# The first feed-forward product of three tile pairs as seven block products in place of eight

## The chip, the core and the metric

The kernel runs on one core of one Trainium2 chip. The metric is the device time of one execution in microseconds (us). Five engines work side by side, each through a program of its own in fixed order: TensorE (PE; its weight loads are shown as PEld), VectorE (DVE), ScalarE (ACT), GpSimd (POOL) and SyncE (SP, which here issues DMAs). They wait for one another on semaphores. TensorE writes its products to PSUM, eight banks of 128 partitions x 512 float32; the other data lie in SBUF. Lower is better.

## The reference

Attention over normalised queries and keys, a Fourier mixing, a normalisation and a feed-forward layer, for 8 batches of 448 tokens with 12 heads of 64 (768 features, 3072 hidden):

```python
def _attn_ref(q, k, v, tau):
    q_n = q / (np.linalg.norm(q, axis=-1, keepdims=True) + 1e-06)
    k_n = k / (np.linalg.norm(k, axis=-1, keepdims=True) + 1e-06)
    scores = np.matmul(q_n, k_n.transpose(0, 1, 3, 2)) / tau
    ...
    return np.matmul(attn, v).astype(np.float32)

def _moe_ref(x, w_ch1, w_ch2):
    X = np.fft.fft(x, axis=1)
    X = np.fft.fft(X, axis=2)
    mixed = np.real(X).astype(np.float32)
    u = x + mixed
    mu = np.mean(u, axis=-1, keepdims=True)
    var = np.mean((u - mu) ** 2, axis=-1, keepdims=True)
    un = (u - mu) / np.sqrt(var + 1e-06)
    ch = np.maximum(un @ w_ch1, 0.0) @ w_ch2
    return (u + ch).astype(np.float32)
```

The change concerns `un @ w_ch1`, called the first product here; the product with `w_ch2` is the second.

## The kernel before

**Planner.** No instruction is written straight to an engine. Each operation is added to a plan (`Plan.add`, L152) with the engines that may run it, a modelled duration, a priority (a lower number goes first) and the names of the buffers that it reads and writes, from which its dependencies follow. `Plan.schedule` (L196) then puts the operations in order on each engine by list scheduling with these modelled times; `emit` (L366) writes them out with the waits. PSUM is handed out in `Tile`s from two pools: "M", two tiles of one bank, and "G", three tiles of two banks. The table `SHIFT` (L39) adds a correction, found beforehand, to the priority of single operations, so that it shapes the order of the whole program. `fill` puts warm-up matmuls into gaps of TensorE.

**Order of the work.** `build` goes through the batches: Fourier mixing of batch b (`fft`, L1039), then attention of batch b+1 (`attn`, L835), then the feed-forward layer of batch b (`ffn`, L1284). The feed-forward matmuls carry priority 5000 + b and each follows the one before (`self.main`), so they form one chain that fills TensorE wherever attention and mixing leave room. After attention of batch 7 and its mixing only this chain is left.

**Tiles.** The symmetry of the transform leaves three or four tiles of 128 tokens a batch. Odd batches have two pairs, even ones (but batch 0) a pair and a single tile. (b, i) below is the pair of batch b that begins with tile i; the last three pairs are (6,0), (7,0) and (7,2), and between (6,0) and (7,0) comes the single tile of batch 6. The normalised tiles lie transposed in `UNT` (6 blocks of 128 features x 4 slots of 128 tokens), put there by DMA transposes on SP's queue (L1147).

**First product.** `up` (L1179) takes units. For a pair a unit is two hidden blocks of 128, each with 6 matmuls (one for each 128 features) whose moving operand is 256 wide (both tiles), 12 matmuls into one bank; 12 units a pair, 144 matmuls. The relu on the way out of PSUM (L1210, on ACT or DVE) writes the bank to `HQ`, quarters 0 to 3: quarter `h + 2t` is half h of the hidden features of tile t. For a single tile a unit is four hidden blocks of 24 matmuls 128 wide.

**Second product.** It is already done with seven block products in place of eight (Strassen-Winograd): sums of weight blocks in `TX` and in place in `W2b` (`sums`, L1364, made once), sums of quarters of `HQ` on DVE (`comb`, L1316: s1 writes the fifth quarter 4 = 2 + 3, s3 writes 2 = 2 - 0, s2 writes 0 = 4 - 0, s4 writes 1 = 1 - 0, each in three parts k), products m1, m2, m6, m5, m7, m3, m4 of 12 matmuls 384 wide (`prod`, L1218, in three parts c), and `fin` (L1238), which moves partial results to the output staging `OUTB` or adds them there. `store` (L1261) sends `OUTB` out, by SP's queue or by an indirect DMA of POOL (L1278).

**Buffers that the change uses.** `STG` (staged queries and keys), `QH` (the same, normalised), `QT` and `KT` (their transposes), `E` (exponentials) belong to the attention, which has ended for batch 7 when the last pairs are computed.

Of the kernel before, what the change touches and what calls it, by code (L numbers as in the profile page):

```python
# [6 lines left out]

AluOp = mybir.AluOpType
# [7 lines left out]
NJ = DM // 128  # L16
# [23 lines left out]
    "iota": {0: -518.9}, "cst": {0: 1028.3}, "tqd": {1: 36.2}, "vz1": {0: 13.5}, "ldt0": {0: 144.7}, "half": {1: -49}, "ldt": {0: 140.9},  # L40
# [53 lines left out]

LATE = {r"W[12]_\d+": 1.5, "tmd": 2.0, r"sq\d_2": 4.0, r"sq\d_\d": 2.0, r"ktd\d": 3.0, r"qdup\d": 3.0, r"qk\d._[2-7]": 1.5, r"pv\d\d_[2-7]": 2.0, r"pv\d\d_1": 1.0, r"h\d+_[1-7]": 0.3}
PIECE = {r"sc[KQ]\d_0": 0.95, r"scT\d_0": 0.42, r"sc\d_\d": 0.6, r"f[avm]\dp_\d": 0.54, r"t\d\d": 0.94}
PORT = r"eps\d|f[a01]\d_\d|g\d_\d|u\d+_\d|un\d_\d|s\d\d_\d|t\d\d|sc[KQT]\d_\d"  # L100
# [1395 lines left out]
```

## Time and profile before

| | us |
|---|---|
| median of 3 runs | 591.05 (590.52 to 591.43) |
| profiled execution | 588.35 |
| its span, first to last instruction | 586.4 |
| busy: PE, PEld | 566.3, 437.5 |
| busy: DVE, ACT, POOL | 416.9, 353.7, 215.1 |
| granted TensorE clock | 0.999 |

How to read it: a group of instructions is shown with its line in the kernel, engine, operation, output and inputs, shape and count, then busy time and the mean duration of one in ns, then the idle time of the engine before it. Durations of matmuls contain a tail that overlaps the next one, so the pace of a stream is read from the chain of waits, where the pieces don't overlap, and not from a mean duration. A window shows the busy time of each engine between two points of time from the span's start.

### The profile page before, as it was taken

Reading aid. Unit: us, or ns where it says so; the run is one execution under the profiler, and the core shown is the slowest. Engines: PE = TensorE matmul, PEld = TensorE weight load, DVE = VectorE, ACT = ScalarE, POOL = GpSimd, SP = SyncE. Lnnn points to the kernel's source line nnn. Section 1 sums busy time; section 2 is a strip of 40 time slices with the busy share of each in tenths; the row PEclk is TensorE's granted clock in tenths of the full one; section 3 lists DMA queues with packets and bytes.
Section 4 is the critical chain, followed back from the end, with each engine's and each line's share of the span. In section 5 each row is a group of like instructions: output and inputs, shape, how many; then the busy total and the mean of one; then the engine's idle time right before and its main releaser. Section 6 shows DMA issues by size and latency. Waiting matters only on the chain.

```text
span 586.4 us, 14876 instructions
## 1 busy us (share of the span) xinstructions
PE 566.3 (97%) x6070; PEld 437.5 (75%) x6070; DVE 416.9 (71%) x971; ACT 353.7 (60%) x681; POOL 215.1 (37%) x318
## 2 busy tenths in 40 slices
PE   3989999999999999999999999999999999999997
PEld 2668788686686786868778687688868778778684
DVE  8989967997679989795899779857944668112222
ACT  7896986257966795478559766784465334124140
POOL 7734424464373527432352652425210120200302
PEclk9999999999999999999999999999999999999999
DMA  9999999865299659745592599249110011110101
GB/s 220 180 218 167 166 185 117 189 141 107 65 165 113 150 110 148 157 68 123 72 172 49 117 171 100 68 113 167 29 39 31 15 55 33 63 42 1 55 1 55
DMA packets 187637, 62.12 MB, mean 106 GB/s; under 512 B 166704, under 2 KB 185392, under 8 KB 187568
## 3 DMA queue, kind: packets, MB, share of 16 engines
q1 hardware_dynamic: 129648, 38.35, 34.1%
q0 software_dynamic: 57920, 22.81, 31.6%
q8 instruction: 48, 0.79, 0.6%
q14 instruction: 21, 0.17, 0.1%
HBM read 51.90 MB, written 11.01 MB: 107 GB/s over the span
## 4 chain that ended last, share of the span: by engine, by line
PE 83%; DVE 9%; DMA 3%; issue 2%; ACT 1%; POOL 1%; SPq 0%; POOLq 0%; DVEq 0%; ACTq 0%
PE PS L1194 35%; PE PS L1225 31%; PE PS L935 5%; PE PS L898 5%; PE PS L1060 2%; PE PS L929 2%; PE PS L1022 2%; DVE U L1088 1%; DMA TX<-in_q_dram 1%; DMA QT<-QH 1%; PE PS L910 1%; DVE QH L717 1%; DVE HQ L1319 1%; ACT E L876 1%; PE PS L911 1%
## 5 line engine op out<-in xcount | busy, mean ns | idle before, releaser
L1194 PE MATMUL PS<-UNT,W1b 128*128 128x256 bf16 (+1 forms) x2304 | 234.2, 259 | 0.4 <-DMA UNT<-F 0.3
L1194 PEld LDWEIGHTS PS<-UNT,W1b 128*128 128x128 bf16 x2304 | 198.8, 98 | 23.0 <-issue 2.6
L876 ACT ACTIVATE E<-PS 128x900 bf16<-128x900 f32 (+1 forms) x192 | 148.0, 827 | 28.0 <-PE PS L898 25.4
L1210 ACT ACTIVATE HQ<-PS 128x512 bf16<-128x512 f32 x129 | 77.0, 597 | 97.8 <-PE PS L1194 96.9
L1225 PE MATMUL PS<-W2b,HQ 128*128 128x384 bf16 x768 | 133.9, 326 | 0.0
L824 POOL TENSOR_TENSOR QH<-STG,SM 128x256 bf16<-128x256 f32 x126 | 84.0, 694 | 97.8 <-DVE SM L633 72.4
L1225 PEld LDWEIGHTS PS<-W2b,HQ 128*128 128x128 bf16 x768 | 73.5, 98 | 46.4 <-issue 2.2
L1319 DVE TENSOR_TENSOR HQ<-HQ 128x512 bf16<-128x512 bf16 x141 | 62.4, 465 | 48.2 <-ACT HQ L1210 44.9
L1249 POOL TENSOR_TENSOR OUTB<-OUTB,U 128x192 f32<-128x192 f32 x66 | 39.8, 624 | 139.5 <-ACT OUTB L1244 138.7
L1225 PE MATMUL PS<-TX,HQ 128*128 128x384 bf16 x396 | 70.9, 326 | 0.2 <-DVE OUTB L1256 0.2
L1225 PEld LDWEIGHTS PS<-TX,HQ 128*128 128x128 bf16 x396 | 37.8, 98 | 24.2 <-issue 0.7
L817 DVE TENSOR_REDUCE SM<-QH 128x6 f32<-128x384 f32 x84 | 44.8, 541 | 10.1 <-ACT QH L815 9.5
L815 ACT ACTIVATE QH<-STG 128x384 f32<-128x384 f32 x84 | 42.5, 519 | 14.6 <-DVE SM L817 9.9
L935 PE MATMUL PS<-VB,E 128*128 128x65 bf16 x1152 | 50.8, 193 | 0.0
L935 PEld LDWEIGHTS PS<-VB,E 128*128 128x128 bf16 x1152 | 47.5, 97 | 1.0
L1278 POOL DMA_INDIRECT out_dram<-OUTB,IDX x20 | 20.6, 1031 | 64.7 <-issue 33.1
L929 PE MATMUL PS<-VZ,E 128*128 128x130 bf16 x192 | 41.6, 219 | 0.3 <-ACT E L876 0.3
L1088 DVE TENSOR_TENSOR U<-ACG,X 128x384 bf16<-128x384 f32 (+3 forms) x70 | 39.6, 590 | 2.2 <-POOL OUTB L1249 1.4
L898 PE MATMUL PS<-QT,KT 64*128 64x225 bf16 x576 | 40.0, 261 | 1.2 <-ACT E L876 0.7
L1256 DVE TENSOR_TENSOR OUTB<-PS,OUTB 128x384 f32<-128x384 f32 x33 | 18.2, 551 | 30.4 <-PE PS L1225 27.0
L1210 DVE TENSOR_SCALAR HQ<-PS 128x512 bf16<-128x512 f32 x33 | 22.7, 687 | 17.9 <-PE PS L1194 17.9
L898 PEld LDWEIGHTS PS<-QT,KT 64*128 64x128 bf16 x576 | 22.7, 94 | 15.8 <-issue 5.4
(134 smaller groups left out, 623.1 us busy)
## 6 DMA issues: line engine op xcount, KB each, us to landing
STG<-in_k_dram SPq DMA_DIRECT2D x18, 384.0 KB, 4.5
STG<-in_q_dram SPq DMA_DIRECT2D x18, 384.0 KB, 3.9
VB<-in_v_dram POOLq DMA_DIRECT2D x24, 192.0 KB, 7.4
W1b<-in_moe_w_ch_dram POOLq DMA_DIRECT2D x12, 384.0 KB, 7.5
W2b<-in_moe_w_ch_dram POOLq DMA_DIRECT2D x12, 384.0 KB, 6.7
out_dram<-OUTB SPq DMA_DIRECT2D x7, 384.0 KB, 2.6
TX<-in_k_dram SPq DMA_DIRECT2D x2, 576.0 KB, 5.5
TX<-in_q_dram SPq DMA_DIRECT2D x2, 576.0 KB, 7.1
```

Of the source, the lines that this page charges most:

```text
L815: P.add("act", lambda a, sq=sq, src=buf[:, w * x:w * x + w]: a.activation(sq, src, ACTF.Square), t_act(w) + 0.034, pr, f"sq{i}_{b}", reads ...
L817: P.add("dve", lambda v, o=SS[:, i, H // ns * x:H // ns * (x + 1)], sq=sq: v.tensor_reduce(o, sq.rearrange("p (h d) -> p h d", d=DH), AX.X ...
L824: r = v.tensor_tensor(v3(qh)[:, h:h + 4], v3(buf)[:, h:h + 4], RN[:, i, h:h + 4].unsqueeze(2).to_broadcast((128, 4, DH)), AluOp.mult)
L876: return a.activation(o, self.PS[:, bk:bk + nc_, 0:SQ2], ACTF.Exp, scale=1.0 / self.tau)
L898: i = pe.matmul(self.PS[:, bk + h, c0:c0 + NK], self.KT[r, jj, kt * 128:(kt + 1) * 128], self.QT[r, jj, cols], start=True, stop=True)
L929: r = pe.matmul(o, st(6), self.VZ[:, j, :], start=not split, stop=(split and i == 0), skip_group_check=True)
L935: r = pe.matmul(o[:, 65 * h:65 * h + 65], st(2 * kt + h), self.VB[:, kt, 2 * j + h, :], start=(split and i == h == kt == 0), stop=((not sp ...
L1088: return v.tensor_tensor(U[o0:o0 + n, ut, cs].rearrange("p (i e) -> p i e", e=2), src, X[i0:i0 + n, x, cs].rearrange("p (i e) -> p i e", e ...
L1194: r = pe.matmul(self.PS[:, bk, x * n:(x + 1) * n], self.W1b[:, j, ft * 128:(ft + 1) * 128], self.UNT[:, j, cs], start=(j == 0), stop=(j == ...
L1210: return e.activation(o, i, ACTF.Relu) if e is self.nc.scalar else e.tensor_relu(o, i)
L1225: r = pe.matmul(self.PS[:, bk, 0:n], lhs(f), rhs(f), start=(start and f == 0), stop=(stop and f == NF // 2 - 1), skip_group_check=True)
L1319: P.add("dve", lambda v: v.tensor_tensor(cs(o), cs(a), cs(bq), op), 0.335, -0.5, f"{nm}{k}_{b}", reads=rd, writes=hr(o)(k))
```

## The change

In the pairs named in `ROUNDS` the first product is also done with seven block products. The blocks are: activations A[t][k], tile t and half k of the 768 features (3 blocks of 128); weights W[k][h], h half of the hidden features. A round r takes hidden blocks 4r to 4r+3 of each half (the work of four units). Pair (6,0) does rounds 0 and 1 so, and its last four units as before; (7,0) and (7,2) do all three rounds.

- `wsums(r)`: three sums of weight blocks, V0 to V2, of 128 x 1536 in buffers of the attention (round 0 in `STG`, 1 in `QH`, 2 in `KT` and `E[1]`), and a fourth in place in `W1b`. Four DVE operations a round, twelve in all.
- `mixed`: four sums of activation blocks, S0 to S3, in the fifth quarter of `HQ`; then the rounds, interleaved by a written sequence. Each product is 12 matmuls 128 wide. In a round the first bank of a G tile gets a1, then a6, a7 and a4 on top, the second a5 and a3, an M tile a2. Between them the bank is copied out (`copy`, float32, on ACT or DVE) and combined (`add`, a custom DVE operation: sum, clipped at 0) into `HQ`.
- `spare`: the buffers of these copies: `OUTB` in three parts, in batch 7 first three parts of `QT`.
- `ffn`: with three rounds the last two products of the third go behind the first and the third part of m1 (`hook`), and s1, s3 are added there.
- `up`: for the single tile of batch 6 the sum A0 + A1 replaces the second half of the activations where the weight was changed in place; the count of matmuls stays.
- `SHIFT` is replaced as a whole, `PORT` (operations that the planner takes to share a port with POOL) has the new names.

```diff
+ROUNDS = {(6, 0): (0, 1), (7, 0): (0, 1, 2), (7, 2): (0, 1, 2)}
+TPRIO = {0: 610, 1: 611, 2: 620}
...
+        if not pair and self.T3:
+            A = self.UNT[:, 0:3, cs], self.UNT[:, 3:6, cs]
+            self.sa(b, 0, lambda v: v.tensor_tensor(self.SA[:, 0], A[0], A[1], AluOp.add), un, True)
...
+    def sa(self, b, x, fn, rd, first=False):
+
+        self.P.add(("dve", "pool"), fn, (0.267, 0.62), -0.5, f"z{x}0_{b}", reads=rd + ([] if first else self.san),
+                   writes=[f"SA{x}"] + (self.san if first else []))
+
+    def mixed(self, b, idx, rounds):
...
+        self.sa(b, 0, tt(SA[:, 0], A[1][0], A[1][1], AluOp.add), un[1], True)
+        self.sa(b, 1, tt(SA[:, 1], SA[:, 0], A[0][0], AluOp.subtract), ["SA0"] + un[0])
+        self.sa(b, 2, tt(SA[:, 2], A[1][0], A[0][0], AluOp.subtract), un[0] + un[1])
+        self.sa(b, 3, tt(SA[:, 3], A[0][1], SA[:, 1], AluOp.subtract), ["SA1"] + un[0])
...
+            def prod(nm, tl, w, a, start, stop, read=None, acq=None):
+                for f in range(0, 4, 2):
+                    def fn(pe, f=f):
+                        for y in (f, f + 1):
+                            for j in range(3):
+                                i = pe.matmul(ps(tl)[:, 128 * y:128 * y + 128], w[0](y, j), a[0](j), start=(start and y == j == 0),
+                                              stop=(stop and y == 3 and j == 2), skip_group_check=True)
+                        return i
+                    self.main = P.add("pe", fn, 6 * t_mm(128), 5000 + b, f"{nm}{r}_{b}", reads=w[1] + a[1], tiles=(tl[0],),
+                                      acquire=acq if f == 0 else None, after=[self.main] + ([read] if read else []))
+                return self.main
+
+            def copy(nm, tl, op):
+                k = free.pop(0)
+                buf, bn = bufs[k]
+                first = bn[0] not in used
+                used.add(bn[0])
+
+                def ev(e):
+                    return e.activation(buf, ps(tl), ACTF.Copy) if e is self.nc.scalar else e.tensor_copy(buf, ps(tl))
+                c = P.add(("act", "dve"), ev, (t_act(512), t_dve(512)), -1, f"{nm}{r}_{b}", reads=[] if first else bn,
+                          writes=[f"CP{k}"] + (bn if first else []), after=(op,), tiles=(tl[0],))
+                return k, c
+
+            def add(nm, q, tl, k, op):
+                free.append(k)
+                return P.add("dve", lambda v: v._custom_dve(TENSOR_ADD_SAT, out=hq(q), in0=ps(tl), in1=bufs[k][0], s0=3.4028235e38, s1=0.0),
+                             t_dve(512), -1, f"{nm}{r}_{b}", reads=bufs[k][1] + [f"CP{k}"], writes=hn(q), after=(op,), tiles=(tl[0],))
+            op = prod("a1", b1, W(0, 0), U_(0, 0), True, False, acq=g)
+            ka, rd = copy("ca", b1, op)
+            yield
+            op = prod("a2", ta, W(1, 0), U_(0, 1), True, True, acq=ta[0])
+            add("ra", 0, ta, ka, op)
+            yield
+            op = prod("a5", tb, V(0), S(0), True, False)
+            kc, rd2 = copy("cc", tb, op)
+            yield
+            op = prod("a6", b1, V(1), S(1), False, False, rd)
+            kb, rd = copy("cb", b1, op)
+            yield
+            op = prod("a3", tb, W(1, 1), S(3), False, True, rd2)
+            add("rb", 1, tb, kb, op)
+            yield
+            op = prod("a7", b1, W(0, 1), S(2), False, False, rd)
+            rd = add("rc", 3, b1, kc, op)
+            yield
+            op = prod("a4", b1, V(2), U_(1, 1), False, True, rd)
...
+        seq = {1: "u u a a a u a a u a u a u u u", 2: "u a a a b b a a b u a b b a u b u b",
+               3: "a a a b b a a b b a b c a c c b c c b"}[len(rounds)].split()
...
+    def spare(self, b):
...
+        bufs = [(o[:, 512 * x:512 * x + 512], ["OUT0", "OUT0b", "OUT1", "OUT1b"]) for x in range(3)]
+        if b == self.nb - 1:
+            q = fl(self.QT[:]).bitcast(F32)
+            names = [f"QT{t}_{j}" for t in range(4) for j in range(NJ)] + [f"QTd_{j}" for j in range(NJ)]
+            bufs = [(q[:, 512 * x:512 * x + 512], names) for x in range(3)] + bufs
+        return bufs
+
+    def wsums(self, r):
...
+        for x, o, a, c, rd, wr in ((1, V[0], B(0, 1), B(0, 0), wn(0) + wn(1), vn(0) + homes[0][1]),
+                                   (2, V[1], B(1, 1), V[0], wn(1) + vn(0), vn(1) + homes[1][1]),
+                                   (4, V[2], B(1, 0), V[1], wn(0) + vn(1), vn(2) + homes[2][1]),
+                                   (3, B(0, 1), B(0, 1), B(1, 1), wn(1), wn(1))):
+            P.add("dve", lambda v, o=o, a=a, c=c: v.tensor_tensor(o, a, c, AluOp.subtract), t_dve(1536, 2), TPRIO[r], f"v{x}{r}", reads=rd, writes=wr)
...
+                if rounds:
+                    rest = self.mixed(b, (i, i + 1), rounds)
+                else:
+                    self.up(b, (i, i + 1), chunks, True)
+
+                def s13(k):
                     comb(4, 2, 3, k, AluOp.add, "s1")
                     comb(2, 2, 0, k, AluOp.subtract, "s3")
+
+                def hook(c):
+                    if c == 0:
+                        next(rest)
+                        for k in range(2):
+                            s13(k)
+                    elif c == 2:
+                        next(rest)
+                        s13(2)
```

The letters of `seq` are the steps in TensorE's order: a, b, c the next product of the first, second, third round, u a unit as before.

More of the change, by code (lines that the diff above doesn't have):

```diff
@@ L6 @@
 from concourse import mybir
+from concourse.dve_ops import TENSOR_ADD_SAT
 AluOp = mybir.AluOpType
@@ L1216, in up, with round_, ev, units @@
             self.evac(ev, 512, -1, f"relu{f0}_{b}", writes=wr, after=(self.main,), tiles=(tile,))
-    def prod(self, b, tile, lhs, rhs, lr, rr, nm, start, stop, read=None, n=384):
+    def sa(self, b, x, fn, rd, first=False):
+        self.P.add(("dve", "pool"), fn, (0.267, 0.62), -0.5, f"z{x}0_{b}", reads=rd + ([] if first else self.san),
+                   writes=[f"SA{x}"] + (self.san if first else []))
+    def mixed(self, b, idx, rounds):
+        P = self.P
+        s0, s1 = [self.slots[b][i] for i in idx]
+        A = [[self.UNT[:, 3 * k:3 * k + 3, 128 * s:128 * s + 128] for k in (0, 1)] for s in (s0, s1)]
+        un = [f"uT{s0}"], [f"uT{s1}"]
+        SA, HH = self.SA, NF // 2
+        tt = lambda o, x, y, op: (lambda v: v.tensor_tensor(o, x, y, op))
+        self.sa(b, 0, tt(SA[:, 0], A[1][0], A[1][1], AluOp.add), un[1], True)
+        self.sa(b, 1, tt(SA[:, 1], SA[:, 0], A[0][0], AluOp.subtract), ["SA0"] + un[0])
+        self.sa(b, 2, tt(SA[:, 2], A[1][0], A[0][0], AluOp.subtract), un[0] + un[1])
+        self.sa(b, 3, tt(SA[:, 3], A[0][1], SA[:, 1], AluOp.subtract), ["SA1"] + un[0])
+        S = lambda x: ((lambda j: SA[:, x, j]), self.san + [f"SA{x}"])
+        U_ = lambda t, k: ((lambda j: A[t][k][:, j]), un[t])
+        bufs = self.spare(b)
+        free, used = list(range(len(bufs))), set()
+        def round_(n, r):
+            g, ta = Tile("G"), Tile("M")
+            b1, tb = (g, 0), (g, 1)
+            ta = (ta, 0)
+            W = lambda k, h: ((lambda f, j: self.W1b[:, 3 * k + j, (HH * h + 4 * r + f) * 128:(HH * h + 4 * r + f) * 128 + 128]),
+                              [f"W1_{6 * h + 2 * r + x}" for x in range(2)])
+            V = lambda x: ((lambda f, j: self.V[r][x][:, j, 128 * f:128 * f + 128]), [f"V{r}{x}"])
+            ps = lambda tl: self.PS[:, self.bank(tl[0]) + tl[1], :]
+            hq = lambda q: self.HQ[:, q, 4 * r:4 * r + 4, :].rearrange("p f c -> p (f c)")
+            hn = lambda q: [f"H{q}_{r}" + x for x in "xy"]
+            def prod(nm, tl, w, a, start, stop, read=None, acq=None):
[42 more added lines that the diff above has]
+            op = prod("a4", b1, V(2), U_(1, 1), False, True, rd)
+            def ev(e):
+                return e.activation(hq(2), ps(b1), ACTF.Relu) if e is self.nc.scalar else e.tensor_relu(hq(2), ps(b1))
+            P.add(("act", "dve"), ev, (t_act(512), t_dve(512)), -1, f"rd{r}r_{b}", writes=hn(2), after=(op,), tiles=(g,))
+            yield
+        def units():
+            for c in range(3):
+                if c not in rounds:
+                    for f in (4 * c, 4 * c + 12, 4 * c + 2, 4 * c + 14):
+                        self.up(b, idx, (f,), True)
+                        yield
+        gens = dict(zip("abc", [round_(n, r) for n, r in enumerate(rounds)]), u=units())
+        seq = {1: "u u a a a u a a u a u a u u u", 2: "u a a a b b a a b u a b b a u b u b",
+               3: "a a a b b a a b b a b c a c c b c c b"}[len(rounds)].split()
+        for x in seq:
+            next(gens[x])
+        return gens["c"] if len(rounds) == 3 else None
@@ new lines, in spare @@
+    def spare(self, b):
+        fl = lambda a: a.rearrange("p a b -> p (a b)")
+        o = fl(self.OUTB[:])
+        bufs = [(o[:, 512 * x:512 * x + 512], ["OUT0", "OUT0b", "OUT1", "OUT1b"]) for x in range(3)]
[4 more added lines that the diff above has]
+        return bufs
@@ L1220, in prod @@
+    def prod(self, b, tile, lhs, rhs, lr, rr, nm, start, stop, read=None, n=384, hook=None):
         P = self.P
@@ L1406, in build @@
         self.snu = []
+        self.SA = self.HQ[:, 4].rearrange("p (s j) c -> p s j c", s=4)
+        self.san = [f"H4_{c}" + x for c in range(3) for x in ("", "x", "y")]
+        self.T3, self.V = set(), {}
         self.consts()
```

40 lines of the change are left out of this document (31 added, 9 removed), and 99 rows, old and new, of the table SHIFT.

## The prediction

> **What bounds the kernel now.** I read the page's first line, then the chain of waits, then the engines by stage, then the rows that price the parts. The page begins:
>
> ```profile
> span 586.4 us, 14876 instructions
> ```
>
> The chain of work that ended last, from 478 us on, merged by line (start, length, what):
>
> ```profile
> 478.69 15.72 PE PS L1194 x144
> 494.42 13.65 PE PS L1225 x84
> 508.07 8.04 PE PS L1194 x144
> 516.11 7.80 PE PS L1225 x48
> 523.91 15.72 PE PS L1194 x144
> 539.63 13.65 PE PS L1225 x84
> 553.28 15.72 PE PS L1194 x144
> 569.00 13.66 PE PS L1225 x84
> 582.68 0.56 DVE OUTB L1256
> ```
>
> From 478.69 to 582.66 us the chain is TensorE alone. L1194 is the first product, L1225 the second. The three runs of 15.72 us are the first products of the last three pairs: (6,0) at 478.69, (7,0) at 523.91, (7,2) at 553.28. The run of 8.04 us is the single tile of batch 6. TensorE's own timeline gives the shapes of these runs:
>
> ```profile
> 478.53 15.88 PE L1194 MATMUL PS<-UNT,W1b 128*128 128x256 bf16 x144
> 507.90 8.20 PE L1194 MATMUL PS<-UNT,W1b 128*128 128x128 bf16 x144
> ```
>
> So a matmul 256 wide costs 15.72/144 = 109.2 ns in the chain, and one 128 wide 8.04/144 = 55.8 ns. Each has its own weight load, and halving the width still halves the time. That decides this case. Now the engines by stage (window, its length, busy us per engine):
>
> ```profile
> 0.00:60.00 60.00, 46.69 (x644) 36.73 (x645) 53.01 (x120) 47.78 (x81) 34.70 (x60) 1.00 1.35 195
> 60.00:583.00 523.00, 519.61 (x5428) 400.81 (x5426) 363.70 (x853) 305.93 (x602) 180.33 (x259) 1.00 0.59 95
> 425.00:440.00 15.00, 15.00 (x158) 10.03 (x157) 6.33 (x15) 10.09 (x16) 2.66 (x5) 1.00 0.14 40
> 440.00:462.00 22.00, 22.00 (x296) 19.27 (x294) 9.22 (x20) 12.53 (x18) 1.07 (x1) 1.00 0.05 20
> 462.00:478.00 16.00, 16.00 (x114) 10.56 (x111) 11.30 (x28) 3.79 (x7) 5.00 (x7) 1.00 0.13 38
> 478.00:494.00 16.00, 16.00 (x151) 14.28 (x149) 14.46 (x35) 8.63 (x21) 0.97 (x1) 1.00 0.06 26
> 494.00:508.00 14.00, 14.00 (x90) 8.54 (x89) 5.29 (x12) 2.15 (x5) 3.34 (x6) 1.00 0.26 54
> 508.00:524.00 16.00, 16.00 (x196) 12.88 (x195) 2.39 (x5) 3.58 (x6) 0.99 (x1) 1.00 0.17 53
> 524.00:540.00 16.00, 16.00 (x148) 14.20 (x146) 2.26 (x5) 6.91 (x12) 0.97 (x1) 1.00 0.07 26
> 553.00:569.00 16.00, 16.00 (x148) 14.24 (x147) 2.26 (x5) 6.58 (x11) 1.67 (x2) 1.00 0.12 50
> ```
>
> The columns after the length, with the number of instructions in brackets, are PE, PEld, DVE, ACT, POOL, granted clock. TensorE is idle for only 523.00 - 519.61 = 3.39 us between 60 and 583. In the stages of batch 7 VectorE works 2.26 of 16 us. In the stage of (6,0) it works 14.46 of 16, because the transform of batch 7 runs there. So: matmul time taken out of the last 105 us comes off the end one for one, if the vector work put in keeps up, and only (6,0) has a VectorE that is nearly full.
>
> **The change, part by part.** *Matmuls.* A round computes four hidden blocks of each half for both tiles of a pair. Before, that is 4 units of 12 matmuls 256 wide: 48 x 109.2 = 5.24 us. After, it is 7 products of 12 matmuls 128 wide: 84 x 55.8 = 4.69 us. Gain 0.554 us a round. There are 2 + 3 + 3 = 8 rounds, so -4.43 us: -1.11 in (6,0), -1.66 in each of the others. The single tile keeps its 144 matmuls.
>
> The row of the weight loads, and a rule against the change:
>
> ```profile
> L1194 PEld LDWEIGHTS PS<-UNT,W1b 128*128 128x128 bf16 x2304 | 198.8, 98 | 23.0 <-issue 2.6
> ```
>
> A load lasts 98 ns, more than a 128-wide matmul's 55.8 ns in the chain, so successive loads must overlap already in the run at 508.07. The Trainium skill, page "TensorE: Matmul & The Clock Gate", section "Back-to-back issue gap", puts a sustained stream of load and matmul pairs 128 wide at about 81 ns each. By that (an estimate) a round would take 84 x 81 = 6.8 us and the change would lose 12.5 us; this trace disagrees with 55.8 ns.
>
> *Evacuations.* A round has three plain copies out of PSUM, one relu and three adds with relu (VectorE only), where four relus stood. No row shows the new add. Nearest rows, from VectorE's groups by form and from the page:
>
> ```profile
> L1256 DVE TENSOR_TENSOR OUTB<-PS,OUTB 128x384 f32<-128x384 f32 x33 | 18.2, 551 | 30.4 <-PE PS L1225 27.0
> L1210 DVE TENSOR_SCALAR HQ<-PS 128x512 bf16<-128x512 f32 x33 | 22.7, 687 | 17.9 <-PE PS L1194 17.9
> L548 DVE SCALAR_TENSOR_TENSOR U<-OUTB,TX,UNT 128x385 f32<-128x385 f32 x2 | 1.1, 605 | 0.0
> L1319 DVE TENSOR_TENSOR HQ<-HQ 128x512 bf16<-128x512 bf16 x141 | 62.4, 465 | 48.2 <-ACT HQ L1210 44.9
> L1210 ACT ACTIVATE HQ<-PS 128x512 bf16<-128x512 f32 x129 | 77.0, 597 | 97.8 <-PE PS L1194 96.9
> ```
>
> Below: 465 ns, the bf16 sum of that length. Above: 605 x 512/385 = 805 ns. I take 0.69, as the relu of the same 512 from PSUM. A copy is like ACT's 0.60.
>
> A relu starts about 0.1 us after its unit (the first unit of (7,0) ends at 523.91 + 12 x 0.1092 = 525.22):
>
> ```profile
> 525.31 0.60 ACT L1210 ACTIVATE HQ<-PS 128x512 bf16<-128x512 f32 x1 [8.57 <-PE PS L1194]
> ```
>
> TensorE waits for these at fixed places, and as it runs in order, every later product queues behind the one that waits. The tightest are the last product of a round, which waits for the add that reads its bank, with two products of 12 between (2 x 0.67 = 1.34 us), and the third product into the second bank, which waits for a copy, also 1.34 us in the worst place. Add: 0.1 us to start, 0.69, say as long back = 0.89, so 0.45 spare. It stalls only if it takes over 1.14 us, or is queued 0.45 us late. In (7,0) and (7,2) VectorE gets 9 x 0.69 = 6.2 us beside 2.26, and ACT keeps 12 x 0.60: cover stands. The combinations now wait for the last round: from the end of its sixth product to the first use of the combined quarter lie two thirds of a second-layer product (1.3, as 12 x 13.65/84 = 1.95), the seventh (0.67) and another second-layer product (1.95), 3.9 us, and 5.2 to the last use, against one add and nine combinations, 0.69 + 9 x 0.465 = 4.9. Just covered; 0 taken, 0.5 a pair if it fails.
>
> In (6,0) 6 x 0.69 = 4.1 us join 14.46: 18.6 in 14.9. The adds go ahead by priority, and 3.7 us of transform move into 494-508, where VectorE is idle 8.7. Batch 7's tiles are due only at 523, and the last of them is normalised at 494 (VectorE's timeline):
>
> ```profile
> 493.70 0.48 DVE L1126 TENSOR_SCALAR F<-U,MV 128x768 bf16<-128x768 bf16 x1 [0.67 <-ACT MV L1123]
> ```
>
> So late transform costs nothing. But each op in VectorE's queue is 0.5 to 0.6 us and orders are fixed beforehand, so an add may stand behind one: bounds 0 and 4 waits (two adds, two copies) of 0.6 = 2.4; I take 0.3, nearer 0, because the 12 relus of this stage all sat on ACT, which was busy only 8.63.
>
> *Copy buffers.* In (6,0) the copies go to the output staging, which the last rows of batch 5 leave by an indirect store. Its issue (POOL's timeline) and its time to landing (all such stores, min/median/max):
>
> ```profile
> 478.70 0.97 POOL L1278 DMA_INDIRECT out_dram<-OUTB,IDX  x1 [2.24 <-issue]
> DMA to landing us min/median/max: 3.0/3.8/7.0
> ```
>
> Landing at 478.70 + 3.8 = 482.5, first copy done 483.2. The product that needs it is the seventh step (one unit 1.31, five products of 0.67): 478.69 + 4.66 = 483.35. So 0 at the median, 3.15 at the maximum; ACT's queue (copies, relus) stands still meanwhile. I take 0.3. In batch 7 three further buffers come first, and the staging is needed only after the seventh product, past the landing.
>
> *Weight sums.* Twelve subtractions of 128x1536. The same shape:
>
> ```profile
> L1380 DVE TENSOR_TENSOR TX<-W2b,TX x6: 893/946/1361, 82.4 to 131.9; 128x1536 bf16<-128x1536 bf16 x6
> ```
>
> 12 x 0.946 = 11.4 us of VectorE, all off the path: 8 of them (7.6) for (6,0) between 425 and 478, where it is idle 8.7 + 12.8 + 4.7 = 26.2 us; 4 (3.8) for (7,0) between 494 and 524, idle 22. The part overwritten in the first weight is free once the pair before has read it. Uncovered, the two in-place ones would cost 1.9. Cost 0.
>
> *Activation sums.* Four of 128x384 a pair, at most 0.465 us each on VectorE. They lie in the fifth hidden quarter, free long before (6,0) and (7,2). For (7,0) it is read up to 523.91, when the finishing add also comes:
>
> ```profile
> 524.01 0.56 DVE L1256 TENSOR_TENSOR OUTB<-PS,U 128x384 f32<-128x384 f32 x1 [3.31 <-PE PS L1225]
> ```
>
> Behind it the first sum ends about 525.04; the product wants it at 523.91 + 1.34 = 525.25. 0 to 0.3; I take 0.1.
>
> *The priority table* is rewritten, which reorders every engine's program. No row prices that. Of idle TensorE it can win at most the 3.39 us after 60 and part of 13.3 before it; by symmetry it can lose as much. I take 0, bounds -3.4 and +3.4.
>
> Sum: -4.43 + 0.3 + 0.3 + 0.1 = -3.73. The profiled execution (588.35 us: span 586.4 and 1.95 around it) would become 584.6. The median of the runs is 2.70 above that execution, so 591.05 - 3.73 = 587.3.
>
> **Rivals.**
> 1. *VectorE bounds (6,0)* (ends slower). All of the stage's vector work comes onto the path: 14.46 + 4.1 + two in-place sums 1.9 + four activation sums 1.9 = 22.4 in 14.6, so 7.8 late; -4.43 + 7.8 = +3.4, 594.4. It decides once over 4.4 us is not deferred. For it: 14.46 of 16. Against: 523 is far off for the transform, and 462-478 has 4.7 idle.
> 2. *The staging lands late* (7.0 us): 3.15 for 0.3, so 590.2. Against: 3.8 is the median.
> 3. *The new order loses* what the old had: 3.4 us, so 590.7, no change. For it: nothing in the rows ties the new order to the old one's 3.39 us of idle. 4. *It wins* 2.3 of them: 585.0.
> 5. *Weight loads pace the products* at their 98 ns: 84 x 98 = 8.2 us a round, +3.0, eight times +24: 615. Against: the run of 8.04 us. The page above is the milder form of this.
>
> **How the numbers follow.** 0.2% is 1.2 us, about what a measurement of this kernel tells from no change. Forecast 0.56 (own range 586.0 to 589.0); VectorE 0.08; staging 0.10; order loses 0.12; order wins 0.11; weight loads 0.03. Faster: 0.56 + 0.11, half the staging case (a landing between) and a quarter of the order's = 0.75. Slower: 0.08 + 0.03 and a fifth of the order case (with idle won back in the first 60 us lost) = 0.13. Same: 0.12. The range 585.0 to 591.0 leaves out the VectorE and weight-load cases and the tails of the order cases, under 2 in 10.
>
> **What would show it.** Right: runs of 84 matmuls 128 wide at 55.8 ns, stages of (7,0) and (7,2) 1.66 us shorter, (6,0) 1.1 less its stalls, TensorE idle before none of the adds or copies, the new add near 690 ns, weight sums near 946 ns between 425 and 478. Wrong: TensorE waiting for VectorE's add or ACT's copy in (6,0), the first copy starting after 483, a 128-wide matmul over 62 ns (84 x 62.4 = 5.24, no gain), or stages before 478 us longer than now.

## The result and the profile after

| us | before | after |
|---|---|---|
| median (lowest to highest, 8 runs each) | 591.3 (587.05 to 593.75) | 585.25 (584.57 to 585.46) |
| ratio, 95% interval | | 0.990 (0.9875 to 0.9925) |
| profiled execution | 588.35 | 585.28 |
| its span | 586.4 | 583.5 |

The change is faster, by 6.0 us in the medians and by 3.07 us between the two profiled executions. The forecast was 587.3, in a range from 585.0 to 591.0. The first line and the engines of the page after:

```profile
span 583.5 us, 15563 instructions
PE 563.0 (96%) x6364; PEld 437.9 (75%) x6364; DVE 445.2 (76%) x1014; ACT 354.5 (61%) x685; POOL 217.8 (37%) x320
```

TensorE is busy 3.3 us less with more instructions, and VectorE 28.3 us more (416.9 before). The chain of waits after, from (6,0)'s second product on (L1361 is now the second product, L1260 the block products, L1197 the units as before; start, length, what):

```profile
493.80 1.96 PE PS L1361 x12
...
496.43 2.12 POOL OUTB L1387 x2
...
505.99 2.12 PE PS L1361 x12
508.11 8.04 PE PS L1197 x144
516.15 7.80 PE PS L1361 x48
523.95 12.73 PE PS L1260 x228
...
539.97 9.76 PE PS L1361 x60
549.76 0.57 DVE OUTB L1394
...
553.36 4.04 DMA out_dram<-OUTB,IDX
557.56 0.61 ACT OUTB L1274
558.21 6.87 PE PS L1260 x120
...
568.37 11.71 PE PS L1361 x72
580.11 0.56 DVE OUTB L1394
```

The reader is to see three things. The stream of 228 block matmuls 128 wide runs through in 12.73 us: 55.8 ns each, the pace on which the forecast was built. From 505.99 to 549.73 nothing but TensorE is on the chain. And two pieces of other engines stand where before there was only TensorE: GpSimd's add at 496.43, which leads to the wait before 505.99, and the landing of a store at 553.36, which holds ACT's copy and with it TensorE until 558.21.

The two waits in the list of TensorE's waits (total, times, longest):

```profile
PE PS L1260 <- ACT OUTB L1274: 0.5, 1, 0.5
...
PE PS L1361 <- DVE OUTB L1394: 0.5, 1, 0.5
```

The end of TensorE's work moves from 582.66 (569.00 + 13.66 before) to 580.08 (568.37 + 11.71), by -2.58 us. Stage by stage: (6,0)'s second product starts at 493.80 for 494.42, -0.62 where the matmuls alone give -1.11, so 0.49 is lost up to there. It lasts 14.31 (to 508.11) for 13.65, +0.66: 0.5 of waiting and the start of the stream behind the wait (its first 12 matmuls take 2.12 for 1.95). The single tile starts at 508.11 for 508.07. (7,0) ends at 551.67 (539.97 + 72 matmuls of 162.5 ns), 27.72 after 523.95 where it took 29.37: -1.65. (7,2) takes 28.41 for 29.38: -0.97, which is -1.66 of matmuls and 0.69 lost at 558.21 (0.5 of waiting, and the next 120 matmuls at 57.3 ns in place of 55.8). Together -4.43 + 0.49 + 0.66 + 0.69 = -2.59.

The 0.49 ahead of (6,0) is not shown to be a price of the change. Long before the first block product, where the second product of (5,0) begins, 0.42 of it is already there (421.08 before, 421.50 after). But in the second pair of profiled executions (experiments 1 and 5) the same point lies at 420.33 and 420.27, and (6,0)'s second product starts 1.16 us earlier after the change (493.67 and 492.51), as much as the matmuls give. Two executions of one kernel differ by more than the 0.49. Behind the end of TensorE the span's tail is 0.32 shorter, and the time outside the span 0.17: -2.58 - 0.32 - 0.17 = -3.07.

The other half of the 6.0 us does not lie between these two executions. The median of before stands 2.95 us above its own profiled execution, the median after (585.25) at its profiled one (585.28). Experiments 1 and 2 turn to that.

The new add and the weight sums, from VectorE's groups by form (count, then busy us, mean ns):

```profile
L1281 DVE CUSTOM_DVE_ANT_0 HQ<-PS,OUTB 128x512 bf16<-128x512 f32 x14 | 9.6, 688 | 6.5 <-ACT OUTB L1274 5.1 <-PE PS L1260 1.2
L1281 DVE CUSTOM_DVE_ANT_0 HQ<-PS,QT 128x512 bf16<-128x512 f32 x10 | 6.9, 691 | 9.3 <-PE PS L1260 7.2 <-ACT QT L1274 2.0
...
L1352 DVE TENSOR_TENSOR W1b<-W1b 128x1536 bf16<-128x1536 bf16 x3 | 2.9, 955 | 1.6 <-PE PS L1197 1.6
```

The 24 adds take 688 to 691 ns (0.69 was taken), the sums of 128x1536 about 0.95 us.

Why TensorE waits at 505.99 is read back along the engines. GpSimd's timeline, before and after:

```profile
496.98 1.23 POOL L1249 TENSOR_TENSOR OUTB<-OUTB,U 128x192 f32<-128x192 f32 x2 [17.30 <-ACT OUTB L1244]
```

```profile
496.43 2.11 POOL L1387 TENSOR_TENSOR OUTB<-OUTB,U 128x192 f32<-128x192 f32 x2 [17.73 <-ACT OUTB L1382]
```

and VectorE's timeline after:

```profile
494.53 3.10 DVE L1457 TENSOR_TENSOR HQ<-HQ 128x512 bf16<-128x512 bf16 x9
498.64 0.56 DVE L1394 TENSOR_TENSOR OUTB<-PS,OUTB 128x384 f32<-128x384 f32 x1 [1.01 <-POOL OUTB L1387]
```

GpSimd's two adds take 2.11 us for 1.23. The finishing add of VectorE stands in its queue behind nine sums, waits 1.01 us for GpSimd, and with it all the transform of batch 7 that is queued behind it; the last finishing add of (6,0), which TensorE needs, comes 0.5 us late.

The window of (6,0)'s first product and that of its second (start and end, length, then busy us of PE, PEld, DVE, ACT, POOL):

```profile
476.20:493.80 17.60, 17.60 (x249) 16.95 (x248) 16.55 (x36) 8.03 (x16) 0.97 (x1) 1.00 0.07 26
493.80:508.10 14.30, 13.82 (x88) 8.19 (x86) 13.00 (x30) 2.57 (x6) 5.64 (x7) 1.00 0.11 21
```

So the transform did move into the second product, as argued: VectorE, 5.29 of 14.00 there before, has 13.00 of 14.30. Little room is left, and an idle 1.01 us is not made up.

### The profile page after: what moved, and what is told of

Read it like the earlier page. It is cut to its first block, busy times and chain, and to the rows that moved or that the text cites. A ratio compares the mean times of both kernels' runs of the same rounds, so it can differ in the third digit from the quotient of the medians.

```text
span 583.5 us, 15563 instructions
## 1 busy us (share of the span) xinstructions
PE 563.0 (96%) x6364; PEld 437.9 (75%) x6364; DVE 445.2 (76%) x1014; ACT 354.5 (61%) x685; POOL 217.8 (37%) x320
## 4 chain that ended last, share of the span: by engine, by line
PE 81%; DVE 12%; ACT 3%; issue 2%; DMA 1%; POOL 1%; POOLq 0%; ACTq 0%; DVEq 0%
PE PS L1361 28%; PE PS L1197 28%; PE PS L934 5%; PE PS L1260 5%; PE PS L897 5%; DVE U L1087 2%; PE PS L928 2%; PE PS L1021 2%; PE PS L1059 2%; DVE HQ L1457 1%; DVE ACG L1116 1%; DVE ACG L971 1%; DVE F L978 1%; PE PS L909 1%; DMA out_dram<-OUTB,IDX 1%
## 5 line engine op out<-in xcount | busy, mean ns | idle before, releaser
L1197 PE MATMUL PS<-UNT,W1b 128*128 128x256 bf16 (+1 forms) x1896 | 193.1, 257 | 0.4 <-ACT HQ L1213 0.4
L1197 PEld LDWEIGHTS PS<-UNT,W1b 128*128 128x128 bf16 x1896 | 160.1, 98 | 18.7 <-issue 2.4
L1361 PE MATMUL PS<-W2b,HQ 128*128 128x384 bf16 x768 | 133.7, 326 | 0.3 <-ACT OUTB L1382 0.3
L1361 PEld LDWEIGHTS PS<-W2b,HQ 128*128 128x128 bf16 x768 | 73.6, 98 | 46.5 <-issue 1.3
L1213 ACT ACTIVATE HQ<-PS 128x512 bf16<-128x512 f32 x98 | 58.4, 596 | 60.1 <-PE PS L1197 59.0
L1387 POOL TENSOR_TENSOR OUTB<-OUTB,U 128x192 f32<-128x192 f32 x66 | 41.4, 650 | 134.8 <-ACT OUTB L1382 133.8
L1361 PE MATMUL PS<-TX,HQ 128*128 128x384 bf16 x396 | 71.4, 326 | 0.5 <-DVE OUTB L1394 0.5
L1457 DVE TENSOR_TENSOR HQ<-HQ 128x512 bf16<-128x512 bf16 x141 | 59.5, 453 | 9.1 <-PE PS L1197 3.6
L1361 PEld LDWEIGHTS PS<-TX,HQ 128*128 128x128 bf16 x396 | 37.4, 98 | 24.5 <-issue 1.1
L855 POOL DMA_DIRECT2D VB<-in_v_dram x24 | 25.2, 1058 | 28.1 <-PE PS L934 20.7
```

Source lines behind the costliest of these rows:

```text
L1197: r = pe.matmul(self.PS[:, bk, x * n:(x + 1) * n], self.W1b[:, j, ft * 128:(ft + 1) * 128], self.SA[:, 0, j - 3] if alt and j > 2 else sel ...
L1213: return e.activation(o, i, ACTF.Relu) if e is self.nc.scalar else e.tensor_relu(o, i)
L1361: r = pe.matmul(self.PS[:, bk, 0:n], lhs(f), rhs(f), start=(start and f == 0), stop=(stop and f == NF // 2 - 1), skip_group_check=True)
L1457: P.add("dve", lambda v: v.tensor_tensor(cs(o), cs(a), cs(bq), op), 0.335, -0.5, f"{nm}{k}_{b}", reads=rd, writes=hr(o)(k))
```

## The experiments

In each, the runs of the kernel before beside it on the same chip gave medians of 588.07 (experiments 1 to 4, 23 runs), 588.30 (5 to 8, 11 runs), 588.04 (9 and 10, 16 runs) and 588.42 (11 and 12, 18 runs), with single executions from 586.4 to 594.6. Only kernels of one such group are compared to a few tenths. Line numbers are each kernel's own.

### 1. The kernel before, unchanged

> The kernel before, unchanged, profiled and timed once more. Theory A (the profiled execution of before, 588.35 us, was a lucky one): a second profile lies near the median of 591.3 and shows, against the first, a wait of some 3 us in one stage, the same work otherwise. Theory B (the 3 us lie outside the span, in the launch): the span stays 586.4 and the time between span and total grows from 1.95 to about 5 us.

Measured: 587.81 us (587.06 to 593.30, 12 runs), ratio 1.0002 (0.9973 to 1.0031); profiled 587.65, span 585.7. Its executions spread over 6 us again. The execution that was profiled is one of the short ones, and it shows no wait of some 3 us that would belong to the long ones. Theory B is out: the three long executions (591.82 to 593.30) have spans of 589.7 to 591.3 us, 2.00 to 2.12 below their totals, and the other nine lie 1.89 to 2.10 below theirs, so the extra time is inside the span. One thing goes with it. In all runs of the experiments eight executions have a granted TensorE clock of 0.991 or less, and each is the longest or second longest of its kernel in its comparison (591.05 us and more). Others ran as long at 0.996 and 0.997. Whether the lower clock makes an execution long, or follows from waits that do, stays open.

### 2. The code of before with the priority table of the change

```diff
 SHIFT = {
-    (the rows of before)
+    (the rows of the change)
```

> The code of before with the priority table of the change. Theory A (the block products give -4.4 less about 1.3 of new waits, and the new order the rest, some -2.7): 588.6 us, ratio about 0.9955. Theory B (the new order is worth nothing, all -5.9 come from the block products): ratio 0.998 to 1.002. Theory C (the table fits the new code alone, and is bad for the old one): ratio above 1.002.

Measured: 588.72 us (588.36 to 590.75, 12 runs), ratio 1.0003 (0.9981 to 1.0024). The table by itself is worth nothing for the old work, as theory B had it. But 11 of the 12 executions lie within 588.36 to 588.97: what the new order does is narrow the spread, at about the time of the old order's ordinary executions.

### 3. The code of the change with the priority table of before

> The block products with the priority table of before. Theory A (block products -3.1 net, the table the rest): about 588, ratio 0.995, with each of the last two pairs 1.1 to 1.7 us shorter in the profile. Theory B (all from the block products): about 585.5, ratio 0.99.

Measured: 595.55 us (594.48 to 596.95, 5 runs), ratio 1.0109 (1.007 to 1.0149), which no theory had: the same block products, 7.5 us slower than before. Its chain, and the wait on the way:

```profile
484.97 4.96 DMA out_dram<-OUTB,IDX
...
490.03 0.61 ACT OUTB L1278
...
490.69 3.50 PE PS L1264 x36
```

```profile
PE PS L1264 <- ACT OUTB L1278: 2.1, 1, 2.1
...
PE PS L1365 <- DVE HQ L1461: 0.8, 2, 0.4
```

The single tile of batch 6 starts at 516.17, against 507.32 in experiment 1, 8.85 us later. Of these 6.03 are lost before (6,0) begins: its first matmul is at 483.81 in TensorE's timeline, at 477.78 in experiment 1. Experiments 10 and 11 turn to them. The rest is lost in (6,0), where the landing of the staging is late: the store of batch 5's rows is issued at 484.97, takes 4.96 us to land, and TensorE waits 2.06 us for the copy behind it. Then it runs at a lower clock. By windows of this trace the granted clock is 1.00 from 487 to 490, 0.76 from 490.69 to 492, 0.50 from 492 to 494, 0.80 from 494 to 496 and 1.00 again behind that; the 36 block matmuls at 490.69 take 3.50 us, where 36 x 55.8 ns are 2.01, and the unit behind them 1.67 for 1.31. So the wait costs 2.06 + 1.49 + 0.36, and with the -1.11 of the matmuls that is 2.80 of the 2.82. Batch 7's combinations are late too, 0.4 us a pair.

### 4. The change, with other copy buffers in (7,0) and (7,2)

```diff
-            bufs = [(q[:, 512 * x:512 * x + 512], names) for x in range(3)] + bufs
+            xf = fl(self.X[:]).bitcast(F32)
+            bufs = [(q[:, 512 * x:512 * x + 512], names) for x in range(3)] + [(xf[:, 512 * x:512 * x + 512], [f"X{j}" for j in range(NJ)]) for x in range(3)]
```

`X` holds the attention's output, which is free by then, so no copy of batch 7 needs the output staging. In the traces VectorE, ScalarE and GpSimd run the same operations in the same order as in the change.

> The changed kernel, but in batch 7 the second three copy buffers lie in X, free since the transform, in place of the output staging, so that no copy waits for a store to land. Theory A (the 0.5 us that TensorE waits at 558.21 come from the store that still reads the staging): the wait is gone, 0.5 to 0.7 us faster than the change, about 584.6. Theory B (the copy is late for ACT's own queue): no difference, 585.25.

Measured: 583.30 us (583.19 to 584.00, 6 runs), ratio 0.9897 (0.9863 to 0.993). The chain from (7,2) on:

```profile
550.72 12.73 PE PS L1260 x228
...
566.74 11.71 PE PS L1362 x72
```

The 228 matmuls of (7,2) now run in one piece, as those of (7,0) do. The pair takes 27.73 us (550.72 to 578.45) for 28.41. The wait was for the staging, and its price is the 0.69 us read from the chain.

### 5. The change again

> The changed kernel, unchanged, beside the kernel before on this chip. Theory A (the size of the gain hangs on where the kernel before falls within its wide spread, 586.4 to 594.0 us on the chip of the last runs, while the change is steady): the change lies at 584 to 585.5 within half a us, the ratio anywhere from 0.99 to 0.995. Theory B (the gain itself is 6 us): ratio 0.990 again.

Measured: 583.81 us (583.38 to 584.64, 6 runs), ratio 0.9918 (0.9899 to 0.9938); profiled 583.88. Both waits are there again, 0.33 us in (6,0) and 0.55 in (7,2). Against the profiled 587.65 of experiment 1 it is 3.77 shorter: (6,0)'s second product starts 1.16 earlier and lasts 0.50 longer (14.15 for 13.65), (7,0) is 1.65 shorter and (7,2) 0.92, which makes -3.23 for the end of TensorE, and the tail and the time outside the span are 0.54 shorter. On this chip the change is 1.4 us faster than in the first comparison, and before 3.0 (588.30 for 591.3), so the ratios agree within their intervals, and the 591 of the first comparison was not before's usual time.

### 6. Block products in batch 7 alone

Experiment 4's kernel with

```diff
-ROUNDS = {(6, 0): (0, 1), (7, 0): (0, 1, 2), (7, 2): (0, 1, 2)}
+ROUNDS = {(7, 0): (0, 1, 2), (7, 2): (0, 1, 2)}
```

> Block products in the two pairs of batch 7 alone, copies in QT and X; pair (6,0) as before, so without the sums of weights and activations that it needs. Theory A (in (6,0) two rounds take 1.11 us off and give 0.5 back in waits): 0.6 us slower than the run with the other buffers. Theory B (the vector work of (6,0) costs more than its 1.11 us): not slower, or faster.

Measured: 584.21 us (583.34 to 584.59, 6 runs), ratio 0.9924 (0.9905 to 0.9944). That is 1.10 us above experiment 8 on the same chip, where (6,0) runs without a wait, and two rounds were priced at 1.11. The two profiled executions differ by only 0.23 (583.34 and 583.11), because the one of experiment 6 comes to (6,0) 0.70 earlier (474.54 for 475.24); in the stage itself the first product, with the transform in between, takes 18.66 us in experiment 6 and 17.56 in experiment 8, again 1.10. Against experiment 4, with its wait in (6,0), there is only another chip to compare with, so what (6,0) is worth with that wait is not settled.

### 7. One add of each round issued twice

Experiment 4's kernel; in batch 7 the add that holds up the round's last product is issued first into a buffer that nobody reads, then into its own:

```diff
+                    for o in ([] if scr is None else [scr]) + [hq(q)]:
+                        i = v._custom_dve(TENSOR_ADD_SAT, out=o, in0=ps(tl), in1=bufs[k][0], s0=3.4028235e38, s1=0.0)
```

> As the run with the other buffers, but in batch 7 the third add of each round, which the last product of the round waits for, runs twice in a row (first into a buffer that nobody reads). Theory A (the spare time there is 0.45 us beyond 0.69): the pair of adds takes 1.38 us, each of the six waits about 0.2 to 0.3 us, together 1.2 to 1.8 us slower. Theory B (the adds are not tight): 0.

Measured: 585.15 us (584.97 to 585.49, 6 runs), ratio 0.994 (0.9921 to 0.9959), 2.04 above experiment 8 on the same chip, of which some 0.3 is (6,0)'s second product (14.10 us for 13.82), which has its wait here. The chain in (7,0):

```profile
522.99 6.71 PE PS L1260 x120
...
529.82 0.13 DVE VB L1291
...
530.42 0.69 DVE HQ L1291
...
531.25 2.85 PE PS L1260 x48
```

TensorE's stream, whole in experiment 4, is cut where the add stands. The pairs take 28.88 and 28.76 us for 27.72 and 27.73: 2.19 for six adds, 0.36 each, somewhat more than the 0.2 to 0.3 expected. The second add takes 0.61 to 0.69 in the chain, so the room that the first one left was by this about 0.3 us, not the 0.45 that the forecast worked out. The term was costed at nothing, and that stands; its cover is thin.

### 8. GpSimd's slow add known to the planner

Experiment 4's kernel; the planner's modelled duration of that one operation is set to what the trace showed:

```diff
-       "pool": {"iota": 1.15,
+       "pool": {r"fa0p_6": 2.1, "iota": 1.15,
```

In the traces of experiments 4 and 8 the order of VectorE, ScalarE and GpSimd differs in one place alone: VectorE's finishing add that waited for GpSimd now stands behind two operations that came after it.

> As the run with the other buffers, but the planner is told that GpSimd's addition to the first staged result of (6,0) takes 2.1 us, as measured, and not 1.12; only two of VectorE's operations change places. Theory A (TensorE's 0.5 us wait before the last product of (6,0) comes from VectorE standing idle about 1 us for GpSimd): the wait shrinks or is gone, 0.3 to 0.5 us faster. Theory B (VectorE is late for its sheer load): the same.

Measured: 583.11 us (582.85 to 583.44, 6 runs), ratio 0.9906 (0.9887 to 0.9925), the fastest of the kernels beside experiment 4. The chain:

```profile
492.80 13.82 PE PS L1362 x84
506.62 8.04 PE PS L1197 x144
```

(6,0)'s second product runs in one piece, 13.82 us for 14.31, and the list of TensorE's waits has none left after 476 us. On the same chip it is 0.70 faster than the change (experiment 5), whose two waits were 0.33 + 0.55 = 0.88.

### 9. The old table up to batch 5, the new rows from batch 6 on

> The changed kernel with a mixed table: the rows of before for all operations of batches 0 to 5, the new rows for batches 6 and 7 and the weight sums. Theory A (what the old table spoils is the order around (6,0), so the new rows of the last two batches mend it): within 1.5 us of the change, about 584 to 585.5. Theory B (the order is set by all batches before, the late rows alone do little): 590 or more, as with the old table.

Measured: 588.08 us (587.35 to 591.05, 10 runs), ratio 1.0004 (0.9985 to 1.0023), between what the two theories had. Chain of waits and TensorE's waits:

```profile
481.25 3.00 DMA out_dram<-OUTB,IDX
...
511.17 8.04 PE PS L1148 x144
519.21 7.80 PE PS L1312 x48
527.01 12.73 PE PS L1211 x228
...
554.73 12.73 PE PS L1211 x228
```

```profile
PE PS L1211 <- DVE HQ L1232: 1.3, 2, 0.8
PE PS L1312 <- DVE HQ L1408: 1.2, 1, 1.2
```

The late rows put batch 7 right: 27.72 us for (7,0) (527.01 to 554.73), with no wait. (6,0) they don't: TensorE waits 1.2 us for combinations of the pair before it (at 476.32), so that (6,0) begins 3.3 us later than in experiment 1 (481.08 for 477.78), and then 1.3 for (6,0)'s new adds; the single tile starts at 511.17. So the old rows of batches 0 to 5 still make VectorE late for (6,0). Which of them do is not shown.

### 10. Batch 7 alone, with the old table

Experiment 6's kernel with the table of before.

> Block products in batch 7 alone, copies in QT and X, whole table of before. Theory A (with the old table the loss sits in (6,0), where copies wait for the store and VectorE is full; batch 7 loses 1.5 of its 3.3 us to late combinations): 1.8 us faster than before, about 586.4. Theory B (the old table loses in batch 7's transform whatever (6,0) does): slower than before, 590 or more.

Measured: 590.20 us (589.55 to 591.27, 7 runs), ratio 1.0031 (1.0017 to 1.0044): slower, though (6,0) does no block products at all. Its single tile starts late:

```profile
512.69 8.04 PE PS L1201 x144
```

at 512.69 against 507.32 in experiment 1. The loss is complete before (6,0): its first product starts at 483.15, against 477.94. VectorE's timeline (in brackets the idle time before, and what ended it) shows where weight sums stand:

```profile
401.03 0.96 DVE L1357 TENSOR_TENSOR QH<-W1b 128x1536 bf16<-128x1536 bf16 x1 [0.87 <-DMA QT<-QH]
...
409.40 0.96 DVE L1357 TENSOR_TENSOR STG<-W1b,STG 128x1536 bf16<-128x1536 bf16 x1 [1.68 <-POOL QH L827]
...
463.64 0.96 DVE L1357 TENSOR_TENSOR KT<-W1b 128x1536 bf16<-128x1536 bf16 x1 [1.07 <-PE PS L901]
```

They wait, at the head of VectorE's queue, for buffers that the attention of batch 7 still uses, and the attention's own vector work stands behind them.

### 11. Experiment 10 with the weight sums behind the transform of batch 7

```diff
-            P.add("dve", ..., reads=rd, writes=wr)
+            P.add("dve", ..., reads=rd, writes=wr, order=self.snu[-1:])
```

> As the run with batch 7 alone and the old table (590.2 us), but all twelve sums of weight blocks are put behind the transform of batch 7 in VectorE's order, into the time where it is idle before (7,0). Theory A (with the old table the loss came from weight sums that stand in VectorE's queue waiting for GpSimd or a transpose to leave their buffer, with attention and transform behind them): the loss before (6,0) is gone and batch 7 keeps 1.9 of its 3.3 us: about 586.2, ratio 0.997 against before. Theory B (the loss is the changed order as such): still 589 to 590.5.

Measured: 587.19 us (585.69 to 592.02, 12 runs), ratio 0.9986 (0.9966 to 1.0006). Against before that is no difference that can be told, but against experiment 10 it is -3.0 in the medians and -5.46 between the profiled executions (591.27 and 585.81), and the stage shows it:

```profile
507.45 8.04 PE PS L1201 x144
```

The single tile starts 5.24 us earlier, at before's own time. The profiled executions are the longest of experiment 10 and the second shortest of experiment 11, so 5.24 is the upper side, and the 3.0 of the medians the safer figure. What has moved is nine of the twelve sums, which no engine needs until 523; the three in place stand behind the single tile's matmuls in both traces. The planner has also moved other work: between the two traces VectorE and ScalarE run other operations, too, in another order from 380 us on, and in experiment 11 VectorE's order is before's own up to 495. So the loss comes from the early sums, but how much of it from the 3.62 us in which they wait, and how much from the order that the planner builds round them, is not separated. The spread of before's executions is back in this kernel.

### 12. Experiment 8 with the third round's sums behind the transform

> As the run with the planner's cost of 2.1 us (the fastest so far), but the third round's four weight sums are put behind the transform of batch 7. Theory A (nothing in the fast order waits for these sums any more): the same, 583.1 within 0.4. Theory B (they still delay the transform before (6,0)): 0.5 to 1.5 us faster.

Measured: 584.06 us (583.50 to 584.21, 6 runs), ratio 0.9923 (0.99 to 0.9946). Not faster than experiment 8 (0.9906, 0.9887 to 0.9925), and 0.95 slower in the medians, on another chip. The chain shows two of the sums in (6,0)'s first product:

```profile
490.06 0.83 DVE KT L1353
...
490.91 0.96 DVE E L1353
```

So the new line does less than was meant. It ties the sums to one operation of the transform, the one planned last, and with this table that one runs early: the first sum starts at 489.97, while other operations of the transform run up to 508. Two of the sums have moved from 469.83 and 474.04 in experiment 8 into the stage of (6,0), and from 488.79 to 508.57 VectorE is on the chain. TensorE ends at 578.73 for 577.91. The run shows two sums on the chain in a stage where VectorE has little room (the planner also moved other operations there); what a place behind the whole transform would do, it does not test. That they are in nobody's way in experiment 8 rests on its list of waits alone.

## Why the prediction was right, and where not

**Matmuls, -4.43: right.** 228 matmuls in 12.73 us are the 55.8 ns that the single tile had shown, and (7,0) became 1.65 us shorter for 1.66 forecast. The rule of some 81 ns for each pair of load and matmul in a sustained stream (the Trainium skill, page "TensorE: Matmul & The Clock Gate", section "Back-to-back issue gap") would have made the 228 last 18.5 us (an estimate); this trace disagrees.

**The new add, 0.69: right.** 688 to 691 ns. Its spare room was mis-sized, 0.3 us (experiment 7) for 0.45, without consequence in the change itself.

**VectorE's order in (6,0), +0.3: 0.66** (0.50 in experiment 5), at another place. The step "late transform costs nothing" failed. The adds were forecast to stand behind other work in the first product; the wait came in the second, from the transform that moved there and from GpSimd's add. Experiment 8 shows the cause: with that add's duration known to the planner, and one operation moved, the wait is gone.

**Staging, +0.3 in (6,0) and 0 in batch 7: it was the other way round.** In (6,0) the store was issued at 477.73 and the copies ran from 481.05, and no matmul waited for them. In (7,2) the step "the staging is needed only after the seventh product, past the landing" failed. GpSimd's timeline around the two places, and ACT's:

```profile
477.73 0.97 POOL L1416 DMA_INDIRECT out_dram<-OUTB,IDX  x1 [3.05 <-DVE F L978]
...
551.56 0.98 POOL L1416 DMA_INDIRECT out_dram<-OUTB,IDX  x1 [2.98 <-issue]
553.36 0.96 POOL L1416 DMA_INDIRECT out_dram<-OUTB,IDX  x1 [0.82 <-DMA out_dram<-OUTB,IDX]
```

```profile
481.05 1.77 ACT L1274 ACTIVATE OUTB<-PS 128x512 f32<-128x512 f32 x3
...
557.56 1.72 ACT L1274 ACTIVATE OUTB<-PS 128x512 f32<-128x512 f32 x3 [2.23 <-DMA out_dram<-OUTB,IDX]
```

For (7,0)'s rows there are two stores, and the second is issued 1.80 us after the first (the timeline puts 0.82 of it down to waiting for a store); its landing, 4.04 us later in the chain (557.40), lets the copy go. The forecast had looked at one store's landing. It costs 0.69 (experiment 4).

**Activation sums, +0.1:** nothing of it is seen; (7,0) lost no more than 0.01.

**Combinations "just covered", 0 or 0.5 a pair:** 0 in the change; 0.4 a pair with the old order (experiment 3).

**Weight sums, 0: true of the change, not of the operation.** The argument counted idle time of VectorE between 425 and 478. In the change eleven of them run between 397 and 481, and VectorE stands idle before two, 0.85 and 1.86 us, without a wait of TensorE behind it. Experiments 10 and 11 show what the argument left out: a sum whose buffer isn't free holds everything behind it in the queue. In the wrong place nine of them, with the order that the planner built round them, cost 3.0 us in the medians and 5.2 at the single tile's start in the two traces.

**The priority table, 0 with bounds of 3.4: right by accident.** It was taken as one more term to be added. It is not: alone it gives nothing (experiment 2, 1.0003), while without it the same block products are slower than before (experiment 3, 1.0109). Under the old order the staging did land late, as the second rival had it, but 6.03 of the 8.85 us were gone before (6,0) began, of which neither that rival nor the one in which VectorE bounds (6,0) speaks; that 595.55 is near the 594.4 of the latter is chance. In the new order (6,0)'s second product started 0.49 us later than the matmuls alone give in one pair of profiled executions, and 0.05 earlier in the other.

**From the profiled execution to the median, +2.70: the step that failed.** The sum itself was near: -3.73 forecast, -3.07 between the profiled executions of the first comparison and -3.77 between those of experiments 5 and 1. In part that is luck: 0.49 and 0.54 of these lie in the tail and outside the span, which no term had, and the end of TensorE moved by -2.58 and -3.23. But the forecast of 584.6 for a profiled execution was the better forecast of the median, 585.25. "The median of the runs is 2.70 above that execution" was carried over as if it were a constant of the kernel; it was how before's widely spread executions fell on that occasion (in the four later comparisons its median is 588.0 to 588.4), and the new order spreads little (experiment 2). That the order narrows the spread is shown; by which wait the old one makes it is not.

## What to carry to other kernels

In a stage that TensorE bounds, counting matmuls at the pace of a stream in the same trace gives the gain to a few hundredths of a us; the rest of the work is to find, for each new operation, what stands behind it in its engine's queue while it waits for its buffer. New work and the order it is put in are one change: test each without the other before adding their prices. Compare one profiled execution with another stage by stage, since their totals also hold what happened before the stage (experiment 6), and don't carry the distance between a profile and a median from one kernel to the next.

## What the runs showed of the hardware

- GpSimd's 2 x (128x192) float32 adds took 2.11 us while VectorE ran nine bf16 sums of 128x512, and 1.05 to 1.23 in the stage before the change. That the two engines disturb each other was not tested by itself.
- An indirect store of output rows took 3.00 to 4.96 us from issue to landing on the chains shown here, and 3.0 to 7.0 in the profile before. The second of two was issued 1.80 us after the first, so a buffer that two of them read comes free late: issued at 551.56 and 553.36, free at 557.40.
- In experiment 3 the granted TensorE clock was 1.00 before a wait of 2.06 us, and 0.76, 0.50 and 0.80 in the windows of the 5.3 us behind it. Behind the two waits of about 0.5 us in the change it stayed at 1.00. How long a wait may be without this is not shown.
- One program's executions can spread over 6 us and more (before: 586.4 to 594.6), where the same code in another order keeps 11 of 12 within 0.6.
